# The first stretch of an attention + rational MLP + soft-MoE kernel: constants, two attention pairs and the first weight conversions put in an order written by hand, loads moved to one queue, one conversion operation moved from ScalarE to GpSimd

## The chip, the core and the metric

The kernel runs on one core of a Trainium2 chip. The metric is the device time in microseconds (us) of one execution; lower is better. The engines are TensorE (PE; PEld is its weight load), VectorE (DVE), ScalarE (ACT), GpSimd (POOL) and SyncE (SP, which here only issues DMA transfers). A name with q behind it (SPq, POOLq, ACTq) is that engine's instruction queue. Each engine takes its instructions strictly in its own order; an instruction whose inputs are not ready holds up everything behind it on that engine.

## What is computed

```python
# attention: 4 batches x 8 heads, 768 tokens in chunks of 32, head size 64
k_full = concat([mem_k, k[c_start - 16 : c_end + 8]])      # 64 keys for each chunk, v alike
a = softmax(q_c @ k_full.T / 8);  out_c = a @ v_full
x = attention output as [3072 tokens, 512]
# rational MLP: w_in 512 x 2048, w_out 2048 x 512; both come as float64
h = x @ w_in
g = (a0 + a1*h + a2*h**2 + a3*h**3) / (1 + |b0|*|h| + |b1|*h**2 + 1e-6)
y = g @ w_out
# soft MoE: 8 experts of 4 slots
logits = y @ phi;  slot inputs = softmax over tokens (logits).T @ y
slot outputs = relu(slot @ w1[e]) @ w2[e];  out = softmax over slots (logits) @ slot outputs
```

## The kernel before

The 3072 tokens go in six blocks of 512. A block holds two attention "pairs" of 256 tokens (the tiles `q`, `k`, `v`). For one pair PE makes the scores (L162), DVE takes the row maximum and subtracts it (L180, L183), ACT takes the exponential (L184), DVE sums and inverts (L187 to L189), PE transposes (L197), ACT copies (L199), PE multiplies by v (L207), DVE scales (L217), PE transposes (L226), and ACT and DVE write the result as a high part (L230) and a rest (L231) into the two `xt` tiles of the block. After that a block runs eight steps, one for each 256 columns of `w_in`: PE makes `h` with 24 matmuls (L310), and ACT, DVE and POOL compute the rational function (ACT L527, L528, L530, L546, L547; DVE L529, L540, L541, L557, L558; POOL L504). PE then transposes the result and adds the logits. There are 48 such steps; L529 is the first DVE instruction of a step and occurs once in each.

The two float64 weight matrices arrive as pairs of 32-bit words in eight chunks each, 1 MB a chunk, in staging tiles `g` (four buffers). The word i0 to i7 means the load of a chunk of `w_in`, o0 to o7 one of `w_out`. A conversion to float32 (`f64_narrow`) scales the low word (ACT L269), clips the high word (DVE L270), shifts its exponent (ACT L271) and joins both (DVE L272). For `w_in` (`split_w`, s0 to s7) ACT then makes the high part (L293) and DVE the rest (L294), into `win` tiles. For `w_out` (`narrow_w_out`, n0 to n7) the result goes to a scratch tile and from there to DRAM by a transfer that POOL issues (L301); PE and ACT then form its product with `phi` (w0 to w7: L405, L406; z0 to z7: L413, L414).

All conversions lie ahead of block 0 and in its eight steps. `KN['pre']` lists the work ahead of the first `h`: A and B are slices of the attention of pairs 0 and 1, the other words are loads and conversions. `KN['ord0']` lists the parts of a step of block 0 (s2, for instance, converts the chunk two steps ahead). The emission order gives priorities; a scheduler builds each engine's order from them.

The loads i0, i1, o0, o1 and all q, k, v loads are issued by SP; the later i and o loads by POOL (L280, L285), behind the stores of L301 in POOL's order.

Of the kernel before, what the change touches and what calls it, by code (L numbers as in the profile page):

```python
# [12 lines left out]
AF = mybir.ActivationFunctionType  # L13
ALU = mybir.AluOpType
AX = mybir.AxisListType
U32 = mybir.dt.uint32
# [3 lines left out]
def float_of_bits(u):  # L20
# [1 line left out]


KN = {
    'pre': "q0 i0 v0 q1 o0 v1 i1 o1 s0 A A A A A A A A A A n0 B B B B B B B B B B A A A A A A B B w0 B B B B i2 s1 o2 n1 z0 q2 v2 i3".split(),
    'ord0': "at a1 w1 s2 h0 d1 at t o3 z1 i4 n2 at a2 h1 p0 at p1 at at".split(),
    'ord': "at a1 h0 d1 at t a2 x2 h1 p0 p1 x1 at x3 at at".split(),
    'ordz': "d0 a1 t d1 a2 p0 p1".split(),
# [14 lines left out]
def tile_chunk_attention__rational__soft_moe(  # L43
# [15 lines left out]
    PE, ACT, DVE, POOL, SP = nc.tensor, nc.scalar, nc.vector, nc.gpsimd, nc.sync  # L59

    NPAIR, P, HP, _ = qw.shape
# [5 lines left out]
    NE, _, EFF = w1.shape  # L67
# [15 lines left out]
    LOW = 7.4 / 2.0 ** 32  # L83
    F64_HI = float_of_bits((1150 << 20) | 0xFFFFF)
    w_in = w_in.bitcast(U32)
    w_out = w_out.bitcast(U32)
# [4 lines left out]
    p_T = Pool(ctx.enter_context(tc.tile_pool(name="p_T", bufs=5)))  # L91
# [53 lines left out]
    def attention(pair, tile4=None, after=None):  # L145
        tile4 = tile4 or (lambda shape: p_a4("a4", shape))
        after = pair + 1 if after is None else after
        t_first = 2 * pair
        b = (t_first * P) // BLK
        qt, kt = ahead.pop(("q", pair))  # L150
        if pair < 2:
            both = ps_h("h", [P, 2, 2, HP, WIN])
            sc = [both[:, par] for par in range(2)]
        else:
            sc = [bank([P, 2, HP, WIN]) for _ in range(2)]
        for n in range(2):
            for hp in range(HP):
                for c in range(4):
                    for par in range(2):
                        r = slice(D * par, D * par + D)  # L160
                        o = P * n + CH * c
                        PE.matmul(  # L162
                            sc[par][CH * c:CH * c + CH, n, hp, :],
                            lhsT=qt[r, hp, o:o + CH],
                            rhs=kt[r, hp, 4 * n + c, :],
                            start=True, stop=True)
            yield
        if after < NPAIR:
            load_qk(after)
        pr = tile4([P, 2, HP, 2, WIN])  # L170
        rsum = []
        for par in range(2):
            for n in range(2):
                s0 = ((t_first + n) % TPB) * P
                if s0 == 0:
                    DVE.memset(sc[par][0:CH, n, :, 0:LEFT], NEG)
                if s0 + P == S:
                    DVE.memset(sc[par][P - CH:P, n, :, CTX - RIGHT:CTX], NEG)
            mx = p_sm("mx", [P, 2, HP], bufs=2)
            DVE.tensor_reduce(mx, sc[par], AX.X, ALU.max)  # L180
            yield
            e = pr[:, :, :, par, :]
            DVE.tensor_tensor(e, sc[par], mx.unsqueeze(3).to_broadcast([P, 2, HP, WIN]), ALU.subtract)  # L183
            ACT.activation(e, e, AF.Exp, scale=SCALE)  # L184
            yield
            sm = p_sm("sm", [P, 2, HP], bufs=4)
            DVE.tensor_reduce(sm, e, AX.X, ALU.add)  # L187
            DVE.tensor_scalar(sm, sm, 1e-9, None, ALU.add)
            DVE.reciprocal(sm, sm)  # L189
            rsum.append(sm)  # L190
            yield

        pt = tile4([P, 2, HP, P])
        for n in range(2):
            pb = bank([P, HP, P])
            for hp in range(HP):
                PE.transpose(pb[:, hp, :], pr[:, n, hp].rearrange("p a j -> p (a j)"), ident)  # L197
            yield
            ACT.activation(pt[:, n], pb, AF.Copy)  # L199
        vt = ahead.pop(("v", pair))  # L200
        pv = [bank([P, 2, HP, D]) for _ in range(2)]
        for n in range(2):
            for hp in range(HP):
                for c in range(4):
                    for par in range(2):
                        r = slice(WIN * par, WIN * par + WIN)
                        PE.matmul(  # L207
                            pv[par][CH * c:CH * c + CH, n, hp, :],
                            lhsT=pt[r, n, hp, CH * c:CH * c + CH],
                            rhs=vt[n][r, c, hp, :],  # L210
                            start=True, stop=True)
            if n and after < NPAIR:
                load_v(after)
            yield
        x_tok = tile4([P, 2, HP, 2, D])
        for par in range(2):
            DVE.tensor_tensor(x_tok[:, :, :, par, :], pv[par],  # L217
                              rsum[par].unsqueeze(3).to_broadcast([P, 2, HP, D]), ALU.mult)
            yield

        xh, xl = xt[b]
        for n in range(2):
            o = (P // TT) * ((t_first + n) % TT)
            pb = bank([P, HP, P])
            for hp in range(HP):
                PE.transpose(pb[:, hp, :], x_tok[:, n, hp].rearrange("p a d -> p (a d)"), ident)  # L226
            yield
            src = pb.rearrange("p h (r t) -> p h t r", t=TT)
            th, tl = (x.rearrange("p h (t r) -> p h t r", t=TT)[:, :, :, o:o + P // TT] for x in (xh, xl))
            ACT.activation(th, src, AF.Copy)  # L230
            DVE.tensor_tensor(tl, src, th.bitcast(F32), ALU.subtract)  # L231
            yield

    def attention_block(b):
        new_xt(b)
        for n in range(BLK // (2 * P)):
            yield from attention(b * BLK // (2 * P) + n)

    make_identity(nc, ident)
    ACT.dma_start(out=ctab[:, 0:4], in_=ca.unsqueeze(0).to_broadcast([P, 4]))  # L240
    ACT.dma_start(out=ctab[:, 4:6], in_=cb.unsqueeze(0).to_broadcast([P, 2]))
# [20 lines left out]
    def f64_narrow(dst, src):  # L262

        lo, hi = src[:, :, :, 0], src[:, :, :, 1]
        f = hi.bitcast(F32)
        ACT.activation(lo, lo, AF.Copy, scale=LOW)  # L269
        DVE.tensor_scalar(f, f, -F64_HI, F64_HI, ALU.max, ALU.min)  # L270
        ACT.activation(f, f, AF.Prelu, scale=2.0 ** -112, alpha=-(2.0 ** 32))  # L271
        DVE.scalar_tensor_tensor(dst, hi, 3, lo, ALU.logical_shift_left, ALU.bitwise_or)  # L272

    stage_in, stage_out = {}, {}
    scratch = [p_win("win", [P, 1024]) for _ in range(3)]
# [1 line left out]

    def load_w_in(i):
        t = p_g("g", [P, NC, 2 * P, 2], U32)
        (SP if i < 2 else POOL).dma_start(out=t.rearrange("p c f w -> p c (f w)"), in_=w_in[i])  # L280
        stage_in[i] = t

    def load_w_out(i):
        t = p_g("g", [P, 2, DM, 2], U32)
        (SP if i < 2 else POOL).dma_start(out=t.rearrange("p c f w -> p c (f w)"), in_=w_out[i])  # L285
        stage_out[i] = t

    def split_w(i):
        wh, wl = win[i] = [p_win("win", [P, NC, 2 * P], F32R) for _ in range(2)]
        src = stage_in.pop(i)  # L290
        f64_narrow(src[:, :, :, 1], src)
        f = src[:, :, :, 1].bitcast(F32)
        ACT.activation(wh, f, AF.Copy)  # L293
        DVE.tensor_tensor(wl, f, wh.bitcast(F32), ALU.subtract)  # L294
# [2 lines left out]

    def narrow_w_out(i):
        f = scratch[i % 3].rearrange("p (j d) -> p j d", j=2)
        f64_narrow(f.bitcast(U32), stage_out.pop(i))  # L300
        POOL.dma_start(out=wo_dr[i], in_=f)  # L301
        wo[i] = f

# [117 lines left out]
    def load(what):  # L421
        kind, n = what[0], int(what[1])
        if kind == "q":
            if n == 1:
                load_qk(1, early["q"], early["k"])
            else:
                load_qk(n)
        elif kind == "v":
            load_v(n, [p_S("S", [P, 4, HP, D]) for _ in range(2)] if n == 1 else None)
        elif kind == "i":  # L430
            load_w_in(n)
        elif kind == "o":
            load_w_out(n)

    def convert(what):
        kind, n = what[0], int(what[1])
        if n < NSTEP:
            {"s": split_w, "n": narrow_w_out, "w": wp_chunk, "z": wp_sum, "i": load_w_in, "o": load_w_out}[kind](n)

    new_xt(0)  # L440
    pairs = {"A": attention(0, after=NPAIR), "B": attention(1, lambda shape: p_T("T", shape), after=NPAIR)}
    for what in KN["pre"]:
        if what in pairs:
            next(pairs[what], None)
        elif what[0] in "qmv":
            load(what)
        else:
            convert(what)
    for gen in pairs.values():
        for _ in gen:  # L450
            pass
    total = NBLK * NSTEP
    hs, gt_tile = {}, {}

# [116 lines left out]
    for kk in range(total + 4):  # L571
        b, i = divmod(kk, NSTEP)
# [31 lines left out]
    for n in range(4):  # L604
        for j in range(4):
# [3 lines left out]
                      start=(n == 0), stop=(n == 3))  # L609
# [132 lines left out]
```

## Time and profile before

| | before |
|---|---|
| device time, median of 3 runs | 609.6 us (608.68 to 610.11) |
| the profiled execution: own time / span of its trace | 611.2 / 609.3 us |
| PE, DVE, ACT, POOL busy | 542.0, 450.9, 419.0, 131.0 us |
| granted TensorE clock, mean of the span | 0.959 of full speed |

The span runs from the first instruction to the last of the profiled execution, which as a whole took 1.9 us longer than its span and 1.6 us longer than the median of the timed runs. The busy time of PE counts modelled ends of pipelined matmuls. DMA issue and semaphore instructions are not counted as busy.

### The profile page before, as it was taken

What the parts mean: (1) busy time and instruction counts of PE and PEld (TensorE: products, weight loads), DVE (VectorE), ACT (ScalarE), POOL (GpSimd) and SP (SyncE); (2) the same over time, 40 slices, a digit from 0 to 9 for tenths busy, and PEclk for the clock granted to TensorE, in tenths of its full rate; (3) what the DMA queues carried; (4) which work ended last, traced back from release to release, by engine and by line L of the source; (5) the groups of instructions that cost most, each with busy time, mean ns of one, the idle gap of its engine ahead of it and who ended that gap; (6) DMA issues with size and microseconds to landing.
All of it is one profiled execution on the core that took longest, in us unless ns stands there. A gap on an engine that the chain in (4) does not pass through costs nothing.

```text
span 609.3 us, 13452 instructions
## 1 busy us (share of the span) xinstructions
PE 542.0 (89%) x5832; PEld 380.4 (62%) x5832; DVE 450.9 (74%) x559; ACT 419.0 (69%) x542; POOL 131.0 (21%) x77
## 2 busy tenths in 40 slices
PE   1247999999999999999999999999999998879981
PEld 1236887766776777767777677776777575326220
DVE  3775698985997888979889798897987969710031
ACT  2576799987786787878867778687787869410041
POOL 0111132122331321312313223132233215100000
PEclk9865999999999999999999999999999999788996
DMA  8995953330201322112221032210274344799938
GB/s 304 415 364 236 342 177 121 136 126 35 105 12 61 104 71 105 30 42 105 71 104 49 23 104 72 104 63 10 104 275 161 119 137 161 289 365 400 411 146 335
DMA packets 21755, 97.41 MB, mean 160 GB/s; under 512 B 3136, under 2 KB 3136, under 8 KB 16704
## 3 DMA queue, kind: packets, MB, share of 16 engines
q1 hardware_dynamic: 18000, 79.70, 35.0%
q0 software_dynamic: 2880, 16.78, 7.4%
q8 instruction: 46, 0.75, 0.5%
q10 hardware_dynamic: 816, 0.07, 0.1%
q14 instruction: 13, 0.11, 0.1%
HBM read 86.05 MB, written 10.49 MB: 158 GB/s over the span
## 4 chain that ended last, share of the span: by engine, by line
PE 56%; ACT 12%; DVE 12%; issue 9%; DMA 6%; POOL 2%; DVEq 0%; ACTq 0%; POOLq 0%; SPq 0%
PE h L310 29%; PE m L336 4%; PE m L387 4%; PE lg L329 3%; ACT S L527 3%; DMA g<-in_moe_w_in_dram 3%; ACT S L528 3%; PE m L207 2%; DVE T L540 2%; ACT g L337 2%; PE h L627 2%; PE m L413 2%; POOL S L504 2%; PE m L226 2%; DVE T L541 2%
## 5 line engine op out<-in xcount | busy, mean ns | idle before, releaser
L310 PE MATMUL h<-xt,win 128*128 128x512 f32 x1152 | 292.0, 401 | 0.7 <-DVE T L541 0.6
L310 PEld LDWEIGHTS h<-xt,win 128*128 128x128 f32 x1152 | 209.7, 189 | 46.1 <-DVE T L541 1.4
L504 POOL TENSOR_TENSOR S<-S,S 128x1024 f32<-128x1024 f32 (+1 forms) x49 | 118.1, 2413 | 306.6 <-DVE S L529 282.0
L527 ACT ACTIVATE S<-h,ctab 128x1024 f32<-128x1024 f32 (+1 forms) x49 | 53.8, 1099 | 55.7 <-PE h L310 54.1
L529 DVE SCALAR_TENSOR_TENSOR S<-S,S 128x1024 f32<-128x1024 f32 (+1 forms) x49 | 58.9, 1201 | 40.7 <-ACT S L528 40.6
L540 DVE TENSOR_TENSOR T<-T,h 128x1024 f32<-128x1024 f32 (+1 forms) x49 | 58.4, 1191 | 7.0 <-ACT T L530 7.0
L557 DVE SCALAR_TENSOR_TENSOR T<-T,ctab,S 128x1024 f32<-128x1024 f32 (+1 forms) x49 | 63.3, 1293 | 0.0
L558 DVE SCALAR_TENSOR_TENSOR T<-S,T 128x1024 f32<-128x1024 f32 (+1 forms) x49 | 59.8, 1220 | 3.3 <-POOL S L504 0.5
L336 PEld LDWEIGHTS m<-ident,T 128*128 128x128 f32 x384 | 44.3, 144 | 28.2 <-issue 13.8
L541 DVE SCALAR_TENSOR_TENSOR T<-T,ctab,h 128x1024 f32<-128x1024 f32 (+1 forms) x49 | 61.1, 1246 | 1.1 <-DVE T L540 0.4
L530 ACT ACTIVATE T<-h,ctab 128x1024 f32<-128x1024 f32 (+1 forms) x49 | 59.2, 1208 | 0.0
L337 ACT ACTIVATE g<-m 128x512 f32<-128x512 f32 x96 | 53.6, 603 | 6.4 <-PE m L336 5.2
L546 ACT ACTIVATE S<-S 128x1024 f32<-128x1024 f32 (+1 forms) x49 | 51.7, 1056 | 8.6 <-DVE S L529 5.1
L547 ACT ACTIVATE S<-S,ctab 128x1024 f32<-128x1024 f32 (+1 forms) x49 | 55.9, 1141 | 0.8
L336 PE MATMUL m<-ident,T 128*128 128x128 f32 x384 | 54.1, 281 | 1.2 <-DVE a L183 1.2
L528 ACT ACTIVATE S<-h,ctab 128x1024 f32<-128x1024 f32 (+1 forms) x49 | 54.1, 1105 | 0.4 <-DVE T L557 0.4
L329 PE MATMUL lg<-T,wp 128*32 128x512 f32 x192 | 38.5, 618 | 3.9 <-DVE T L558 3.8
L231 DVE TENSOR_TENSOR xt<-m,xt 128x512 fp32r<-128x512 f32 x24 | 16.5, 688 | 13.9 <-ACT xt L230 13.9
L387 PE MATMUL m<-g,ptok 128*32 128x512 f32 x192 | 23.5, 634 | 0.4 <-ACT ptok L379 0.4
L269 ACT ACTIVATE g<-g 128x1024 uint32<-128x1024 uint32 x16 | 18.6, 1161 | 6.5 <-DMA g<-in_moe_w_in_dram 5.0
L680 DVE TENSOR_SCALAR win<-h,csum 128x512 f32<-128x512 f32 x12 | 8.0, 744 | 20.3 <-PE m L674 20.3
L184 ACT ACTIVATE a<-a 128x512 f32<-128x512 f32 x22 | 14.0, 636 | 12.6 <-DVE a L183 12.6
(154 smaller groups left out, 611.7 us busy)
## 6 DMA issues: line engine op xcount, KB each, us to landing
win<-in_moe_w_dram SPq DMA_DIRECT2D x32, 512.0 KB, 4.9
k<-in_kw_dram SPq DMA_DIRECT2D x11, 1024.0 KB, 7.0
v<-in_vw_dram SPq DMA_DIRECT2D x11, 1024.0 KB, 4.9
g<-in_moe_w_in_dram POOLq DMA_DIRECT2D x6, 1024.0 KB, 7.8
g<-in_moe_w_out_dram POOLq DMA_DIRECT2D x6, 1024.0 KB, 9.6
out_dram<-win SPq DMA_DIRECT2D x12, 512.0 KB, 6.2
q<-in_qw_dram SPq DMA_DIRECT2D x11, 512.0 KB, 3.8
T<-in_moe_w_dram SPq DMA_DIRECT2D x10, 512.0 KB, 10.0
```

Source lines behind the costliest of these rows:

```text
L310: PE.matmul(tile_[:, f2, :], lhsT=ww[:, c, f2 * P:f2 * P + P], rhs=xx[:, c, :], start=(n == 0), stop=(n == 3 * NC - 1))
L336: PE.transpose(pb[:, m, f2 * P:f2 * P + P], t_[:, f2, tt * P:tt * P + P], ident)
L337: ACT.activation(gts[b, qd][:, 2 * part:2 * part + 2, 2 * P * o:2 * P * o + 2 * P], pb, AF.Copy)
L504: POOL.tensor_tensor(out[:, o], q[:, o], w[:, o], ALU.mult)
L527: ACT.activation(s[:, o], hh[:, o], AF.Abs, scale=b0)
L528: ACT.activation(y[:, o], hh[:, o], AF.Square, scale=rb1)
L529: DVE.scalar_tensor_tensor(s[:, o], y[:, o], QC, s[:, o], ALU.add, ALU.add)
L530: ACT.activation(t[:, o], hh[:, o], AF.Identity, bias=a2, scale=a3)
L540: DVE.tensor_tensor(t[:, o], t[:, o], hh[:, o], ALU.mult)
L541: behind[kk] = DVE.scalar_tensor_tensor(t[:, o], t[:, o], a1, hh[:, o], ALU.add, ALU.mult).ins
L557: DVE.scalar_tensor_tensor(t[:, o], t[:, o], a0, w[:, o], ALU.add, ALU.mult)
L558: DVE.scalar_tensor_tensor(t[:, o], e[:, o], 2.0, t[:, o], ALU.subtract, ALU.mult, reverse0=True)
```

## The change

It has four parts. First, everything from the constants to the first `h` is written in a fixed order for PE, ACT, DVE and POOL (`manual_schedule`), in which the slices of pairs 0 and 1 (A, B), the conversion s0 (s) and n0 (n) stand as `KN['pre']` lists them. The conversions became generators for that, in two slices each. What remains of the old list (s1, w0, z0, n1 and the loads i2, o2, i3) is `KN['pre2']`, behind the fixed part and left to the scheduler. Second, the first loads are issued in the order of `KN['loads']`, and all i and o loads are issued by SP. Third, the low words are scaled by POOL in place of ACT, in all 16 conversions. Fourth, in every attention pair the two row sums come after both exponentials.

```diff
 KN = {
-    'pre': "q0 i0 v0 q1 o0 v1 i1 o1 s0 A A A A A A A A A A n0 B B B B B B B B B B A A A A A A B B w0 B B B B i2 s1 o2 n1 z0 q2 v2 i3".split(),
+    'loads': "q0 q1 v0 i0 v1 o0 i1 o1 q2 v2".split(),
+    'pre': "A A B B A A A A A A A A A A B B B B s B B B B A A B B s A A A A s n B B n B B B B".split(),
+    'pre2': "s1 i2 w0 z0 o2 n1 i3".split(),
...
             ACT.activation(e, e, AF.Exp, scale=SCALE)
             yield
+        for par in range(2):
             sm = p_sm("sm", [P, 2, HP], bufs=4)
-            DVE.tensor_reduce(sm, e, AX.X, ALU.add)
+            DVE.tensor_reduce(sm, pr[:, :, :, par, :], AX.X, ALU.add)
...
+    start = ExitStack()
+    start.enter_context(tc.manual_schedule(engines={e.engine for e in (PE, ACT, DVE, POOL)}))
     make_identity(nc, ident)
...
-        ACT.activation(lo, lo, AF.Copy, scale=LOW)
+        POOL.tensor_scalar(lo, lo, LOW, None, ALU.mult)
         DVE.tensor_scalar(f, f, -F64_HI, F64_HI, ALU.max, ALU.min)
         ACT.activation(f, f, AF.Prelu, scale=2.0 ** -112, alpha=-(2.0 ** 32))
+        yield
         DVE.scalar_tensor_tensor(dst, hi, 3, lo, ALU.logical_shift_left, ALU.bitwise_or)
+        yield
...
-        (SP if i < 2 else POOL).dma_start(out=t.rearrange("p c f w -> p c (f w)"), in_=w_in[i])
+        SP.dma_start(out=t.rearrange("p c f w -> p c (f w)"), in_=w_in[i])
...
-        (SP if i < 2 else POOL).dma_start(out=t.rearrange("p c f w -> p c (f w)"), in_=w_out[i])
+        SP.dma_start(out=t.rearrange("p c f w -> p c (f w)"), in_=w_out[i])
...
     new_xt(0)
-    pairs = {"A": attention(0, after=NPAIR), "B": attention(1, lambda shape: p_T("T", shape), after=NPAIR)}
+    for what in KN["loads"]:
+        load(what)
+    gens = {"A": attention(0, after=NPAIR), "B": attention(1, lambda shape: p_T("T", shape), after=NPAIR),
+            "s": split_w(0), "n": narrow_w_out(0)}
     for what in KN["pre"]:
-        if what in pairs:
-            next(pairs[what], None)
-        elif what[0] in "qmv":
-            load(what)
-        else:
-            convert(what)
-    for gen in pairs.values():
+        next(gens[what], None)
+    for gen in gens.values():
         for _ in gen:
             pass
+    start.close()
+    for what in KN["pre2"]:
+        load(what) if what[0] in "qv" else convert(what)
```

The lines move down by 2 to 9 in the changed kernel: L269 becomes L274 (now on POOL), L270 L275, L271 L276, L272 L278, L293 L300, L294 L301, L301 L308, L310 L317, L217 L220, L230 L233, L231 L234, L406 L413, L414 L421, L504 L513, L527 L536, L529 L538.

ACT's order before, from the middle of the first stretch to the high parts of `xt` (L230 into xt_3; a4 and T are the probabilities of pairs 0 and 1; g_5 holds chunk i2, g_6 o2, g_7 i3):

```order
L269 ACTIVATE g_5_540<-g_5_540 128x1024
L271 ACTIVATE g_5_540<-g_5_540 128x1024
L269 ACTIVATE g_6_550<-g_6_550 128x1024
L230 ACTIVATE xt_3_148<-m_7_443 128x16x32
L293 ACTIVATE win_8_670<-g_5_540 128x1024
L271 ACTIVATE g_6_550<-g_6_550 128x1024
L269 ACTIVATE g_7_573<-g_7_573 128x1024
L406 ACTIVATE S_3_517<-m_10_518 128x512
L406 ACTIVATE S_3_517<-m_11_524 128x512
L230 ACTIVATE xt_3_148<-m_12_533 128x16x32
L271 ACTIVATE g_7_573<-g_7_573 128x1024
L414 ACTIVATE wp_4_106<-m_13_557 128x64
```

The last two L230 stand behind the last row. ACT's order now, at the same place (g_1 holds i0, g_2 o0, g_3 i1):

```order
L202 ACTIVATE T_2_428<-m_5_429 128x512
L202 ACTIVATE T_2_428<-m_6_435 128x512
L233 ACTIVATE xt_3_150<-m_9_511 128x16x32
L233 ACTIVATE xt_3_150<-m_10_518 128x16x32
L300 ACTIVATE win_4_415<-g_1_160 128x1024
L276 ACTIVATE g_3_168<-g_3_168 128x1024
L276 ACTIVATE g_2_166<-g_2_166 128x1024
L233 ACTIVATE xt_3_150<-m_11_534 128x16x32
L233 ACTIVATE xt_3_150<-m_12_541 128x16x32
```

All four high parts stand ahead of every operation on i2, o2 and i3, which are no longer ahead of them at all; o0 and i1 still are.

DVE's order now, from pair 0's scaling to the first instruction of step 0 (L538):

```order
L278 SCALAR_TENSOR_TENSOR g_1_160<-g_1_160 128x1024
L234 TENSOR_TENSOR xt_4_151<-m_9_511,xt_3_150 128x16x32
L275 TENSOR_SCALAR g_3_168<-g_3_168 128x1024
L234 TENSOR_TENSOR xt_4_151<-m_10_518,xt_3_150 128x16x32
L301 TENSOR_TENSOR win_5_416<-g_1_160,win_4_415 128x1024
L275 TENSOR_SCALAR g_2_166<-g_2_166 128x1024
L220 TENSOR_TENSOR T_3_530<-m_7_444,sm_7_420 128x8x64
L220 TENSOR_TENSOR T_3_530<-m_8_445,sm_8_424 128x8x64
L278 SCALAR_TENSOR_TENSOR win_1_145<-g_2_166 128x1024
L278 SCALAR_TENSOR_TENSOR g_3_168<-g_3_168 128x1024
L234 TENSOR_TENSOR xt_4_151<-m_11_534,xt_3_150 128x16x32
L234 TENSOR_TENSOR xt_4_151<-m_12_541,xt_3_150 128x16x32
```

The last L234 ends the inputs of the first `h`. Counted to step 0's L538, DVE has done 13 conversion instructions (6 clips, 5 joins, 2 rests) of the 40 that all chunks need; before, 24 (10, 9 and 5) stood ahead of step 0's L529. So 27 are left for the steps of block 0 (10 clips, 11 joins, 6 rests) where 16 were (6, 7 and 3), and 10 scalings are left for POOL.

POOL's order now, in the first steps of block 0 (S are the operands of the multiplication of L513, win the scratch tiles that L308 stores):

```order
L274 TENSOR_SCALAR g_7_590<-g_7_590 128x1024
L274 TENSOR_SCALAR g_8_728<-g_8_728 128x1024
L308 DMA wo_1_144<-win_3_147 128x1024
L274 TENSOR_SCALAR g_9_740<-g_9_740 128x1024
L513 TENSOR_TENSOR S_9_783<-S_4_653,S_7_755 128x1024
L274 TENSOR_SCALAR g_10_831<-g_10_831 128x1024
L308 DMA wo_1_144<-win_1_145 128x1024
L513 TENSOR_TENSOR S_13_950<-S_8_781,S_11_856 128x1024
```

Each step of block 0 now has two scalings beside the one multiplication and the one store; the load issues are gone from POOL.

## Rows read from the trace of the kernel before

**Rows 1.** Page: busy us, share of the span and instructions by engine.

```profile
PE 542.0 (89%) x5832; PEld 380.4 (62%) x5832; DVE 450.9 (74%) x559; ACT 419.0 (69%) x542; POOL 131.0 (21%) x77
```

**Rows 2.** Stages: start:end, length, busy us (instructions) per engine, clock, DMA share, GB/s.

```profile
30.00:40.00 10.00, 3.77 (x136) 3.28 (x136) 6.57 (x11) 7.76 (x9) 0.69 (x2) 0.67 0.99 400
50.00:60.00 10.00, 10.00 (x76) 8.32 (x78) 5.42 (x7) 6.77 (x10) 0.00 (x0) 0.50 0.44 180
```

**Rows 3.** Chain that ended last, in order of time: start us, us, what.

```profile
26.58 0.58 POOL wo L301
...
27.30 9.27 DMA g<-in_moe_w_in_dram
...
38.72 8.55 DMA g<-in_moe_w_in_dram
...
47.36 1.17 ACT g L269
...
57.44 2.43 PE h L310 x5
```

**Rows 4.** Timeline: start us, us, engine, line, operation, out<-in, idle before and releaser.

```profile
8.99 2.04 PE L162 MATMUL h<-k,q 64*32 64x64 f32 x128 [8.99 <-DMA k<-in_kw_dram]
18.79 0.33 SPq L280 DMA_DIRECT2D g<-in_moe_w_in_dram  x1
19.12 0.42 PE L162 MATMUL h<-xt,xt 64*32 64x64 f32 x2 [8.09 <-DMA xt<-in_kw_dram]
21.59 0.70 DVE L270 TENSOR_SCALAR g<-g 128x1024 f32<-128x1024 f32 x1 [0.18 <-DMA g<-in_moe_w_out_dram]
50.86 3.62 PE L413 MATMUL m<-u,S 128*128 128x32 f32 x16
67.81 1.23 DVE L529 SCALAR_TENSOR_TENSOR S<-S,S 128x1024 f32<-128x1024 f32 x1 [2.02 <-ACT S L528]
151.73 1.23 DVE L529 SCALAR_TENSOR_TENSOR S<-S,S 128x1024 f32<-128x1024 f32 x1 [3.38 <-ACT S L528]
```

**Rows 5.** Who waited, SP's queue: total us, times, longest us.

```profile
SPq L280 <- DMA u<-in_moe_phi_dram: 9.1, 1, 9.1
```

**Rows 6.** Stages as in Rows 2: step 0 to step 7, and block 1.

```profile
67.81:151.73 83.92, 80.39 (x877) 62.72 (x876) 71.76 (x82) 73.47 (x96) 19.47 (x13) 1.00 0.41 148
148.59:232.16 83.57, 83.30 (x941) 60.60 (x947) 70.22 (x82) 65.49 (x83) 21.67 (x9) 1.00 0.19 64
```

**Rows 7.** Groups by line and shape: count, busy us, mean ns, idle before.

```profile
L504 POOL TENSOR_TENSOR S<-S,S 128x1024 f32<-128x1024 f32 x47 | 115.1, 2451 | 300.0 <-DVE S L529 282.0 <-DVE sm L189 10.5 <-DVE ce L368 7.5
L269 ACT ACTIVATE g<-g 128x1024 uint32<-128x1024 uint32 x16 | 18.6, 1161 | 6.5 <-DMA g<-in_moe_w_in_dram 5.0 <-DMA g<-in_moe_w_out_dram 1.5
L270 DVE TENSOR_SCALAR g<-g 128x1024 f32<-128x1024 f32 x16 | 11.0, 690 | 3.5 <-DMA g<-in_moe_w_in_dram 3.3 <-DMA g<-in_moe_w_out_dram 0.2
L272 DVE SCALAR_TENSOR_TENSOR g<-g 128x1024 uint32<-128x1024 uint32 x8 | 9.8, 1222 | 1.1 <-ACT g L271 1.0
```

**Rows 8.** One line, L617: min/median/max ns.

```profile
L617 POOL MEMSET a<- x1: 952/952/952, 544.0 to 544.0; 128x1024 f32 x1
```

**Rows 9.** Timeline as in Rows 4, three meetings of DVE and POOL.

```profile
79.90 1.22 DVE L540 TENSOR_TENSOR T<-T,h 128x1024 f32<-128x1024 f32 x1
80.07 2.39 POOL L504 TENSOR_TENSOR S<-S,S 128x1024 f32<-128x1024 f32 x1 [0.67 <-DVE S L529]
81.03 1.46 DVE L188 TENSOR_SCALAR sm<-sm 128x8 f32<-128x8 f32 x1
...
123.66 2.71 POOL L504 TENSOR_TENSOR S<-S,S 128x1024 f32<-128x1024 f32 x1 [4.89 <-DVE S L529]
124.44 3.01 DVE L272 SCALAR_TENSOR_TENSOR win<-g 128x1024 uint32<-128x1024 uint32 x1 [0.34 <-ACT g L271]
...
142.14 1.22 DVE L294 TENSOR_TENSOR win<-g,win 128x1024 fp32r<-128x1024 f32 x1
142.38 3.23 POOL L504 TENSOR_TENSOR S<-S,S 128x1024 f32<-128x1024 f32 x1 [5.47 <-DVE S L529]
```

More of the change, by code (lines that the diff above doesn't have):

```diff
@@ L290, in split_w @@
         src = stage_in.pop(i)
-        f64_narrow(src[:, :, :, 1], src)
+        yield from f64_narrow(src[:, :, :, 1], src)
         f = src[:, :, :, 1].bitcast(F32)
@@ L299, in narrow_w_out @@
         f = scratch[i % 3].rearrange("p (j d) -> p j d", j=2)
-        f64_narrow(f.bitcast(U32), stage_out.pop(i))
+        yield from f64_narrow(f.bitcast(U32), stage_out.pop(i))
         POOL.dma_start(out=wo_dr[i], in_=f)
@@ L437, in convert @@
         if n < NSTEP:
-            {"s": split_w, "n": narrow_w_out, "w": wp_chunk, "z": wp_sum, "i": load_w_in, "o": load_w_out}[kind](n)
+            for _ in {"s": split_w, "n": narrow_w_out, "w": wp_chunk, "z": wp_sum, "i": load_w_in, "o": load_w_out}[kind](n) or ():
+                pass
     new_xt(0)
-    pairs = {"A": attention(0, after=NPAIR), "B": attention(1, lambda shape: p_T("T", shape), after=NPAIR)}
+    for what in KN["loads"]:
+        load(what)
+    gens = {"A": attention(0, after=NPAIR), "B": attention(1, lambda shape: p_T("T", shape), after=NPAIR),
+            "s": split_w(0), "n": narrow_w_out(0)}
     for what in KN["pre"]:
-        if what in pairs:
-            next(pairs[what], None)
-        elif what[0] in "qmv":
-            load(what)
-        else:
-            convert(what)
-    for gen in pairs.values():
+        next(gens[what], None)
+    for gen in gens.values():
         for _ in gen:
             pass
+    start.close()
+    for what in KN["pre2"]:
+        load(what) if what[0] in "qv" else convert(what)
     total = NBLK * NSTEP
```

## The prediction

> **What bounds the kernel now.** I read the page first. PE is busy 542.0 of 609.3 us and DVE 450.9 [rows 1], so a gain must come where PE does not work. The stages show where: from 30 to 40 us PE is busy 3.77 of 10, and the first matmul of `h` starts at 57.4 [rows 2, 3]. The chain of waits tells why. POOL issues its first store only at 26.58, because DVE has not joined o0 sooner; chunk i2, behind it on POOL, then takes 9.27 us to land, chunk i3, issued at 38.72, another 8.55, and ACT L269 on i3 runs at 47.36 [rows 3]. None of that is needed by the first `h`, but on ACT and DVE these operations stand ahead of the last pieces of `xt`. The reader is to see a stretch that waits for transfers of later steps.
>
> From step 0's L529 at 67.81 to step 7's at 151.73 [rows 4] it is another picture: of 83.92 us PE is busy 80.39, ACT 73.47 and DVE 71.76 [rows 6]. Block 1 has PE busy 83.30 of 83.57 [rows 6]. From step 0 on PE sets the pace, with DVE at 86% in block 0. Whatever is won ahead of step 0 shifts all that follows, unless block 0 gets longer.
>
> **When step 0 can come.** The transfers set the earliest times. With 1.57 MB (q0, k0) landed PE starts at 8.99, with 5.24 MB queued up to k1 at 19.12, with o0 as the next 1.05 MB DVE starts at 21.59 [rows 4]: 2.5 us for each further MB. The bytes up to a place in the new order give k1 13, v0 16, i0 19, v1 21.6, o0 24, i1 27, as estimates from these rows. The issue of i1 waits for the small table of `phi` as before (9.1 us, issued at 18.79 [rows 4, 5]); by then 7.3 MB stand ahead of it, so I add nothing.
>
> On DVE pair 0's maxima, subtractions and sums go from 11 to 16, pair 1's to about 23 with the clip of i0 between, which comes at 19 and may stand behind POOL's scaling of i0. The scaling of pair 0 follows at 23 to 25. PE then does pair 1's product with v and the four groups of transposes; the rest is a ladder of ACT copies and DVE subtractions of 0.6 to 0.7 us each, with the clips and joins of i0, i1 and o0 between (0.69 and 1.22 us each [rows 7]). All of it lies behind i1's landing at 27. Counting the rows of DVE's and ACT's new order one behind the other, the last `xt` piece is ready at 37 to 38. I take 38 for the first `h` in place of 57.4, 19.4 us sooner, with 36 and 42 as ends.
>
> From there to L529 it took 10.4 us (57.4 to 67.81 [rows 3, 4]). Now w0 and z0, done earlier before, stand between the matmuls of step 0; z0's sixteen took 3.62 us at the low clock [rows 4] (0.50 of full, which is 1.2 GHz, from 50 to 60 [rows 2]), and some thirty small score matmuls of pair 2 move out from between them. I add 2.4. Step 0's L538 comes at about 51, **17 us sooner** (13 to 20).
>
> **What block 0 gives back.** The conversions that were done in the 57 us of waiting come later now: in DVE's new order 10 clips, 11 joins and 6 rests are left behind step 0's L538, where 6, 7 and 3 were. These are 4 x 0.69 and 7 x 1.22 [rows 7] = 11.3 us more; back to back they overlap by 0.1 each, so 10.4. DVE's 71.76 become 82.2 of 83.9. ACT loses seven L269 and gains four L271 and three L293, each about 1.16 [rows 7]: nothing. PE does the same.
>
> Then the scalings on POOL, 10 of them in this stretch. The trace has no such operation. Below it lies a POOL write of 1024 elements without a read, 0.95 us [rows 8]; above it one with two reads, 2.45 us [rows 7]. One read and one write lie between: 1.7. POOL has room (19.47 busy of 83.92 [rows 6], 36 then), and twelve load issues leave it. But POOL and DVE hold each other up. DVE L188, an operation on 8 elements a row, took 1.46 and ended at 82.49, as POOL's multiplication at 82.46; the join at 124.44 took 3.01, its own 1.22 behind the end of a multiplication at 126.37; and POOL's at 142.38 took 3.23, since L294 ran to 143.36 [rows 9]. L540, which reads one operand from PSUM, kept its 1.22 beside the first of these multiplications [rows 9]. I take the clip, the join and the rest for such operations, and L529, L557 and L558 too: 10 x 0.69, 17 x 1.22 and 21 x 1.23 [rows 4, 7] are about two thirds of the 82.2. A scaling that comes at a random moment waits or makes DVE wait; I put half its time on DVE, 0.85 us each, 8.5 in all. The ends are nothing (it falls beside L540 and L541 or an idle DVE) and all of 2.45.
>
> The Trainium skill, SBUF — State Buffer, section "SBUF: two separate sides", says that a DVE operation with two SBUF inputs or in a two-port mode and a GpSimd operation exclude each other for the whole instruction. The three meetings agree with it; by the rule alone each scaling could cost DVE its full length, which is the rival below that ends slower. The GPSIMD Engine Reference of the Trainium skill, section "Engine selection", calls one-input operations roughly line-rate; from its 1.2 GHz that would be an estimate of 0.85 us for 1024 elements, and at half of it the give-back would be some 4 us smaller. No row here shows a one-input operation of this size.
>
> DVE needs 82.2 + 8.5 = 90.7 then, more than PE's 80.4, and sets the pace. It will not run without a gap, PE needed 4% more than its busy time; I take 92. Block 0 gives back 92 - 84 = **8 us**.
>
> **The other edits.** The sums behind both exponentials take as many instructions in as many slices; they fill DVE while ACT works, in steps where PE is the bound (83.30 of 83.57 in block 1 [rows 6]): nothing. The joins now also wait for POOL; queued behind a late scaling are a store and the multiplication of L513, for which the end of a step waits. Scalings start when their chunk lands, and the slots of `g` come free about a step (10 us) ahead of use, so I cost this at nothing; without that lead each would put its own 1.7 us and a wait for landing on the step. On SP the loads now stand behind q3, k3 and v3, which wait for PE's use of pair 2; the same step of lead covers them, and without it a load's landing, about 9 us [rows 3], would fall on the step.
>
> **Sum.** 17 sooner less 8 is 9. The profiled execution took 611.2 (span 609.3 and 1.9 around it), so it would take 602.2, the span 600.3. The median of the runs is 1.6 below the profiled one: **600.6 us**.
>
> **Rivals.**
> 1. *The scalings are cheap* (25%). If a scaling is near 0.95 us and finds DVE in its PSUM operations, DVE stays near 84 and PE keeps the pace. For it: L540 was not held up [rows 9]. Against it: DVE then is at 98%. Block 0 gives back 1 to 2: 594, between 591 and 596.
> 2. *The scalings stop DVE* (10%). One mechanism: DVE's clip, join or first step operation stands behind every scaling for its whole length. At 2.45 us each DVE needs 82.2 + 24.5 = 106.7, block 0 gives back 22.8, and the time is 615. It decides from 17 = 82.2 + 10x - 83.9, x = 1.87 us each. For it: two of the three meetings are of this kind [rows 9]. Against it: POOL also waits for DVE, and a multiplication, longer by every row, kept DVE only in part.
> 3. *Step 0 hardly comes sooner* (10%). DVE's fixed order has the clip of i1 ahead of pair 0's last piece and that of o0 ahead of pair 1's scaling. If i1 lands at 33 instead of 27, everything behind it moves 6 us: 17 becomes 11, and the time 606.6. For it: fixed orders cannot step around a late transfer. Against it: as many bytes stand ahead of i1 as before.
>
> **Numbers.** The main case has 55%, 597 to 605. The range leaves out the far side of rival 2 and the lower edge of rival 1: 591 to 608.5. A measurement of this kernel tells some 0.2% from no change, so faster means below 608.4. The main case, rival 1 and nearly all of rival 3 are faster, 0.90; 0.03 lie within 0.2%; rival 2 from its point on and a late start together with it are slower, 0.07.
>
> **What would show it.** In the changed kernel's trace: L317 starting near 38 and step 0's L538 near 51; no wait of ACT or DVE for i2 or i3 ahead of it; L274 between 0.95 and 2.45 us; from step 0's to step 7's L538 some 92 us, with DVE busy over 95% and DVE operations of twice their length beside L274; block 1 as long as before. I am wrong if that stretch stays at 84 or goes beyond 101, or if L317 starts after 45.

## The result, and the profile after

The change made the kernel slower: 614.36 us (median of 4 runs, 613.47 to 615.21) against 609.86 (4 runs, 608.68 to 610.18), a ratio of 1.0084 with a 95% interval of 1.0072 to 1.0096. The forecast, 600.6 us and faster, was wrong in sign; 614.36 lies outside its range. The profiled execution took 614.46 us, with a span of 612.7.

The page of the changed kernel, busy time by engine, answers to [rows 1]:

```profile
PE 544.5 (89%) x5832; PEld 382.3 (62%) x5832; DVE 461.4 (75%) x559; ACT 403.0 (66%) x526; POOL 177.3 (29%) x81
```

POOL has 46 us more and ACT 16 less, as the edit says; DVE has 10.5 more with the same 559 instructions. The timeline of the changed kernel, with the first `h` matmul and the first DVE instruction of steps 0 and 7, answers to [rows 4]:

```profile
41.31 0.80 PE L317 MATMUL h<-xt,win 128*128 128x512 f32 x1
...
52.23 1.21 DVE L538 SCALAR_TENSOR_TENSOR S<-S,S 128x1024 f32<-128x1024 f32 x1
...
155.46 1.23 DVE L538 SCALAR_TENSOR_TENSOR S<-S,S 128x1024 f32<-128x1024 f32 x1 [4.79 <-ACT S L537]
```

Step 0 comes 15.6 us sooner (67.81 before), step 7 comes 3.7 us later (151.73 before). Everything that was won ahead of step 0 is lost between these two rows, and more. The stages of the changed kernel, columns as in [rows 2]: from step 0 to step 7 (called the stretch from here on), and on to the first instruction of the last step:

```profile
52.23:155.46 103.23, 88.37 (x879) 68.38 (x878) 88.78 (x93) 74.24 (x96) 54.08 (x23) 0.93 0.48 166
155.46:525.02 369.56, 361.79 (x3846) 262.52 (x3844) 318.39 (x360) 289.03 (x367) 99.59 (x41) 1.00 0.27 93
```

The stretch takes 103.23 us where it took 83.92 [rows 6]. The rest, 369.56, hardly moved: before, 368.86 from step 7's L529 at 151.73 to the last at 520.59. In the stretch DVE executes 93 instructions (82 before) and is busy 88.78 us, close to the 90.7 of the forecast; yet the stretch is 103, not 92. The scaling itself, one line over the whole kernel:

```profile
L274 POOL TENSOR_SCALAR g<-g x16: 2874/3010/3982, 19.3 to 128.7; 128x1024 uint32<-128x1024 uint32 x16
```

Its median of 3.01 us lies above the bracket of 0.95 to 2.45. Three meetings of it with DVE, from the timeline of the changed kernel:

```profile
62.27 1.22 DVE L538 SCALAR_TENSOR_TENSOR S<-S,S 128x1024 f32<-128x1024 f32 x1
62.65 3.63 POOL L274 TENSOR_SCALAR g<-g 128x1024 uint32<-128x1024 uint32 x1 [2.22 <-ACT a L186]
...
99.17 2.97 POOL L274 TENSOR_SCALAR g<-g 128x1024 uint32<-128x1024 uint32 x1
101.22 1.23 DVE L301 TENSOR_TENSOR win<-g,win 128x1024 fp32r<-128x1024 f32 x1 [3.16 <-ACT win L300]
...
108.42 2.95 POOL L274 TENSOR_SCALAR g<-g 128x1024 uint32<-128x1024 uint32 x1
108.54 2.08 DVE L538 SCALAR_TENSOR_TENSOR S<-S,S 128x1024 f32<-128x1024 f32 x1
```

At 62.65 the scaling takes 0.6 us more than its median beside L538, which had begun; at 101.22 L301, with two operands in SBUF, keeps its 1.23 us inside a scaling; at 108.54 L538 is held up for 0.86 and ends at 110.62, before the scaling does (111.37). Either side can pay, with a part of the other's length or with nothing. The Trainium skill, SBUF — State Buffer, section "SBUF: two separate sides", gives whichever of the two begins first the shared port for the whole instruction. The first meeting can be read so; the other two, by their recorded spans, differ from it, and the measurement decides here.

The waits of the changed kernel in the stretch, by engine and line (us in total, times, longest us):

```profile
ACT S L555 <- POOL S L513: 7.9, 4, 3.1
...
PE h L317 <- ACT win L300: 3.7, 3, 2.0
```

Before, L546 (now L555) waited 3.5 us for the multiplication in the stretch, and no `h` matmul for `win`. Rows of the chain that ended last in the changed kernel, in order of time as in [rows 3]:

```profile
77.44 9.01 DMA g<-in_moe_w_out_dram
...
86.59 2.94 POOL g L274
...
95.70 1.84 POOL S L513
...
111.45 2.37 POOL S L513
...
127.86 6.73 DMA wo<-win
```

From the load at 77.44 to L555's start at 113.84 the chain lies on that load and on POOL's order alone: four scalings, two stores and two multiplications, with the gaps between them. In the two longest gaps (1.9 and 5.6 us) a store waited for a join on DVE. The last row is a store. Its join ended on DVE at 125.69; the store stands behind L513 in POOL's order, goes out at 127.86 and takes 6.73 us, and the next high part (L300) waits 3.1 us for the `win` slot that the store reads. In all, 23.4 us of the stretch's chain are on POOL, 15.7 on transfers, 20.5 on PE, 15.7 on ACT, 13.6 on DVE, and for 14.4, those two gaps among them, the chain names no engine.

### The profile page after: what moved, and what is told of

It is laid out like the page before. It is cut to its first block, busy times and chain, and to the rows that moved or that the text cites. A ratio compares the mean times of both kernels' runs of the same rounds, so it can differ in the third digit from the quotient of the medians.

```text
span 612.7 us, 13472 instructions
## 1 busy us (share of the span) xinstructions
PE 544.5 (89%) x5832; PEld 382.3 (62%) x5832; DVE 461.4 (75%) x559; ACT 403.0 (66%) x526; POOL 177.3 (29%) x81
## 4 chain that ended last, share of the span: by engine, by line
PE 49%; DVE 13%; ACT 13%; DMA 9%; issue 7%; POOL 6%; SPq 0%; DVEq 0%; ACTq 0%; POOLq 0%
PE h L317 26%; PE m L394 4%; POOL S L513 3%; ACT S L536 3%; PE m L343 3%; DMA win<-in_moe_w_dram 3%; PE m L210 3%; ACT g L344 3%; ACT S L537 3%; PE lg L336 3%; DVE T L549 2%; POOL g L274 2%; PE m L229 2%; PE m L200 2%; DMA xt<-in_kw_dram 2%
## 5 line engine op out<-in xcount | busy, mean ns | idle before, releaser
L317 PE MATMUL h<-xt,win 128*128 128x512 f32 x1152 | 294.0, 404 | 4.7 <-ACT win L300 3.7
L317 PEld LDWEIGHTS h<-xt,win 128*128 128x128 f32 x1152 | 212.3, 191 | 51.8 <-ACT win L300 5.0
L513 POOL TENSOR_TENSOR S<-S,S 128x1024 f32<-128x1024 f32 (+1 forms) x49 | 119.0, 2431 | 296.1 <-DVE S L538 289.3
L536 ACT ACTIVATE S<-h,ctab 128x1024 f32<-128x1024 f32 (+1 forms) x49 | 53.8, 1099 | 62.3 <-PE h L317 60.3
L538 DVE SCALAR_TENSOR_TENSOR S<-S,S 128x1024 f32<-128x1024 f32 (+1 forms) x49 | 59.6, 1217 | 40.4 <-ACT S L537 40.2
L555 ACT ACTIVATE S<-S 128x1024 f32<-128x1024 f32 (+1 forms) x49 | 51.7, 1054 | 12.9 <-POOL S L513 7.9
L274 POOL TENSOR_SCALAR g<-g 128x1024 uint32<-128x1024 uint32 x16 | 51.5, 3221 | 25.2 <-DMA g<-in_moe_w_in_dram 18.0
L234 DVE TENSOR_TENSOR xt<-m,xt 128x512 fp32r<-128x512 f32 x24 | 16.4, 687 | 13.0 <-ACT xt L233 13.0
L210 PE MATMUL m<-v,a 64*32 64x64 f32 x1408 | 21.8, 236 | 4.2 <-issue 2.5
L210 PEld LDWEIGHTS m<-v,a 64*32 64x32 f32 x1408 | 18.1, 112 | 9.1 <-issue 4.8
```

The lines of the kernel that those rows point to most:

```text
L274: POOL.tensor_scalar(lo, lo, LOW, None, ALU.mult)
L317: PE.matmul(tile_[:, f2, :], lhsT=ww[:, c, f2 * P:f2 * P + P], rhs=xx[:, c, :], start=(n == 0), stop=(n == 3 * NC - 1))
L513: POOL.tensor_tensor(out[:, o], q[:, o], w[:, o], ALU.mult)
L536: ACT.activation(s[:, o], hh[:, o], AF.Abs, scale=b0)
L538: DVE.scalar_tensor_tensor(s[:, o], y[:, o], QC, s[:, o], ALU.add, ALU.add)
```

## The experiments

All 14 kernels ran on a chip beside the kernel before, whose median was between 608.7 and 609.2 in each batch. "Stretch" and busy times are those of one profiled execution. The kernels marked * spread by 1.2% to 1.7% between executions, e5 and e13 by about 1%, so a stretch of theirs is good to a few us. The profiled execution of e5 was 4.1 us above its median, that of e11 2.5 above, that of e6 2.3 below. "Fuller" is the larger busy share of DVE and ACT in the stretch.

| kernel | median us | ratio, 95% interval | step 0 at | stretch | PE / DVE / ACT busy in it | fuller |
|---|---|---|---|---|---|---|
| before | | | 67.81 | 83.92 | 80.39 / 71.76 / 73.47 | ACT 0.88 |
| after | 614.36 | 1.0084 [1.0072, 1.0096] | 52.23 | 103.23 | 88.37 / 88.78 / 74.24 | DVE 0.86 |
| e1_act_scale | 608.21 | 0.9985 [0.9967, 1.0004] | 52.81 | 95.58 | 87.33 / 83.07 / 84.63 | ACT 0.89 |
| e2_before_pool | 616.37 | 1.0122 [1.0096, 1.0149] | 60.79 | 96.79 | 87.18 / 78.04 / 69.20 | DVE 0.81 |
| e3_hybrid | 608.45 | 0.9988 [0.9971, 1.0005] | 52.76 | 97.96 | 89.16 / 83.64 / 84.63 | ACT 0.86 |
| e5_dve_shift | 615.82 | 1.0121 [1.0075, 1.0168] | 57.17 | 103.43 | 92.01 / 90.31 / 74.49 | DVE 0.87 |
| e7_no_clip * | 607.29 | 0.9959 [0.9929, 0.9989] | 52.68 | 94.58 | 86.07 / 75.64 / 85.44 | ACT 0.90 |
| e8_no_scale | 605.57 | 0.9939 [0.9919, 0.9959] | 52.34 | 92.12 | 85.15 / 84.45 / 74.20 | DVE 0.92 |
| e6_act_poolloads * | 605.78 | 0.9942 [0.9912, 0.9972] | 53.00 | 90.99 | 85.11 / 80.72 / 82.45 | ACT 0.91 |
| e10_before_noclip | 603.93 | 0.9917 [0.9892, 0.9942] | 64.74 | 79.84 | 78.54 / 66.19 / 72.75 | ACT 0.91 |
| e11_pool_both | 622.46 | 1.0222 [1.0187, 1.0257] | 54.53 | 110.56 | 91.86 / 88.19 / 73.17 | DVE 0.80 |
| e12_before_sp | 606.56 | 0.9963 [0.9939, 0.9987] | 58.95 | 89.97 | 85.58 / 79.89 / 79.06 | DVE 0.89 |
| e13_sums_before | 603.87 | 0.9917 [0.9888, 0.9947] | 53.28 | 92.62 | 84.66 / 81.53 / 81.49 | DVE 0.88 |
| e14_poolloads_noclip | 602.28 | 0.9894 [0.9878, 0.9911] | 51.49 | 88.86 | 82.60 / 72.78 / 82.50 | ACT 0.93 |
| e16_neither | 600.66 | 0.9858 [0.9838, 0.9878] | 51.98 | 87.27 | 85.24 / 74.46 / 73.28 | DVE 0.85 |
| e15_before_2scale * | 614.28 | 1.0079 [1.0047, 1.0111] | 63.47 | 93.43 | 84.48 / 74.10 / 84.50 | ACT 0.90 |

**The scaling or the conversions left over.** The first theory, P, was that the scalings on POOL cause the loss; its rival, L, that the conversions left for block 0 do. e1 takes the scaling back to ACT and keeps the rest of the change:

```diff
-        POOL.tensor_scalar(lo, lo, LOW, None, ALU.mult)
+        ACT.activation(lo, lo, AF.Copy, scale=LOW)
```

> The changed kernel with the low words scaled by ACT again (part three undone, all else kept). Theory P (the ten 3.0 us scalings on POOL make block 0 long, by POOL's order and by stopping DVE): step 0's L538 stays near 52 us, the stretch to step 7's falls from 103 to between 84 and 95 (DVE 82 + 4, ACT 74 + 12), the time is 596 to 607. Theory L (27 conversion instructions of DVE left for block 0 make it long on whatever engine the scaling is): the stretch stays above 99 and the time is 611 to 615.

e2 makes the opposite edit in the kernel before and nothing else. e3 leaves POOL only the scalings of s0 and n0 in the fixed part. e5 puts the scaling on DVE as a shift to the right (it cuts off where the scaling rounds):

```diff
-        POOL.tensor_scalar(lo, lo, LOW, None, ALU.mult)
+        DVE.tensor_scalar(lo, lo, 29, None, ALU.logical_shift_right)
```

> The kernel before with only the scaling moved to POOL (part three alone). Theory P: the first matmul of h moves little or comes a few us later, the stretch from step 0's L529 to step 7's grows from 84 to 90 or more, the time is 616 to 625. Theory L: the order before leaves 16 conversion instructions for block 0 and has ACT relieved, so the stretch stays within 3 us of 84 and the time is 607 to 612.

> The changed kernel with POOL scaling only s0 and n0 in the fixed part, ACT all 14 later chunks. Theory P: as with ACT alone, within 3 us, since POOL has no other work so early: 595 to 607, no POOL operation but L513's in block 0. Theory L: 611 to 615.

> The changed kernel with the low words brought to three bits by DVE, with a shift right by 29 in place of the scaling (it cuts off where the scaling rounds). POOL is as free as with ACT, DVE has ten more instructions of 0.7 to 1.2 us in block 0. Theory P: DVE then sets the pace with 82 + 4 + 7 to 12, the stretch is 93 to 99, the time 602 to 609. Theory L: DVE's load is what counts, the stretch is over 103 and the time 614 or more. The duration of the shift is also looked for.

Both theories hold in part: e2 came out as P said, e5 as L said, e1 and e3 just outside P's ranges. Without POOL's scalings the stretch still takes 95.58 us, 11.7 more than before, at 608.21 us: all else in the change together is worth nothing that can be measured. POOL's scalings add another 7.6 us, and alone they make the kernel before slower by 1.2%, though step 0 comes 7.0 us sooner there, which no theory had. In the fixed part they are free: e3 equals e1.

With e1's instruction count within one, DVE is busy 88.78 - 83.07 = 5.7 us longer in the changed kernel: about 0.6 us for each of the ten scalings. In e5 POOL scales nothing, DVE does 90.31 us of work, and the stretch is as long as in the changed kernel, in an execution 4.1 us above the median. Here work added to DVE costs about its own length (7.2 us more work than in e1, 7.9 more stretch); the forecast had 92 for 90.7.

**Is it DVE's work alone?** The busy share of DVE was 0.85 to 0.87 in every kernel of these but e2, which suggested that its work sets the stretch (theory D). e7 is e1 without the clip, e10 the kernel before without it:

```diff
-        DVE.tensor_scalar(f, f, -F64_HI, F64_HI, ALU.max, ALU.min)
```

> The changed kernel with ScalarE's scaling of the low words and without VectorE's clip of the high words (the clipping of weights beyond float32's range is left out). It takes 14 clips of about 0.69 us, 9.7 us, from VectorE between step 0's and step 7's L538. Theory D (VectorE's work sets that stretch, at about 0.86 of it busy in every kernel so far): VectorE falls from 83.1 to 73.4 us, the stretch from 95.6 to 85 to 88 us, the time from 608.2 to 598 to 601 us. Theory A (ScalarE's 84.6 us or TensorE's 87.3 us in that stretch set it): the stretch stays at 93 to 96 us, the time at 606 to 609 us.

> The kernel before without VectorE's clip of the high words (the clipping is left out). It takes some 10 clips, 6.9 us, from VectorE between step 0's and step 7's L529. Theory D by its rule of 0.86: VectorE falls from 71.8 to 64.9 us, but TensorE's 80.4 us is a floor, so the stretch goes from 83.9 to 80 to 82 us and the time falls by 2 to 4 us. Theory A (TensorE already sets the kernel before's stretch): the stretch stays at 83 to 84 us, and the time falls by 1 us at most, for the clips ahead of step 0.

e8 is the changed kernel without any scaling; the join reads a zero (`none`) in place of the low word, which is left out:

```diff
+    zero = const("zero", [P, 1])
...
+    POOL.memset(zero, 0.0)
...
-        POOL.tensor_scalar(lo, lo, LOW, None, ALU.mult)
+        none = zero.bitcast(U32).unsqueeze(2).to_broadcast(list(hi.shape))
...
-        DVE.scalar_tensor_tensor(dst, hi, 3, lo, ALU.logical_shift_left, ALU.bitwise_or)
+        DVE.scalar_tensor_tensor(dst, hi, 3, none, ALU.logical_shift_left, ALU.bitwise_or)
```

> The changed kernel with no scaling of the low words at all (the low words are left out; the join reads a zero in their place, with the same VectorE instruction). GpSimd has the load of the kernel before, ScalarE some 10 us less than with its own scaling, VectorE the same conversions. Theory D: the stretch from step 0's to step 7's L538 is as with ScalarE's scaling, 94 to 97 us, and the time 606 to 609 us. Theory A, by ScalarE: the stretch falls to 86 to 90 us and the time to 599 to 603 us.

Theory D fell with e7: DVE lost 7.4 us of the stretch's work, the stretch 1.0. Theory A, by ScalarE alone, fell with e8: ACT lost 10.4, the stretch 3.5 where at least 5.6 was expected. e10 came out just below the lower end of D's stretch (79.84), with PE busy 78.54 of it, and gained 3.1 ahead of step 0 besides; its time fell by 5.0 us for the 2 to 4 expected.

e8 also splits the loss. In the stretch it has the changed kernel's instructions on DVE (93) and ACT (96) and no scaling. It takes 92.12 us, 8.2 more than before: that is what the moved conversions cost, with the loads on SP and the sums as changed. The ten scalings on POOL make the other 11.1 us of the changed kernel's stretch and 8.8 us of its median (614.36 beside 605.57), and DVE is busy only 4.3 us longer with them. In the chain of e8's stretch, as in that of e1's, nothing lies on POOL or on a transfer.

**The queue of the loads.** e6 is e1 with the loads from the third chunk on issued by POOL, e11 the changed kernel with them there, e12 the kernel before with all of them on SP; in both load functions:

```diff
-        SP.dma_start(out=t.rearrange("p c f w -> p c (f w)"), in_=w_in[i])
+        (SP if i < 2 else POOL).dma_start(out=t.rearrange("p c f w -> p c (f w)"), in_=w_in[i])
```

> The changed kernel with ScalarE's scaling and with the weight loads from the third on issued by GpSimd, as in the kernel before. Theory D: the queue does not matter, the stretch is 94 to 97 us and the time 606 to 609 us. Rival Q (loads issued by SP wait behind other work of SP, so conversions come late): the stretch is 90 us or less and the time 603 us or less.

> The changed kernel, GpSimd scaling and all, with the weight loads from the third on issued by GpSimd as in the kernel before. Theory Q (the issue by SP puts the conversions of the next chunks later in the orders that the scheduler builds, so TensorE waits for win, at a cost of its own): the stretch from step 0's to step 7's L538 is 4 to 5 us shorter than in the changed kernel, 98 to 100 us, with no wait of L317 for win, and the time 608 to 611 us. Rival (on GpSimd the loads stand behind the 3.0 us scalings and come as late): the stretch stays at 102 us or more and the time at 613 us or more.

> The kernel before with all weight loads issued by SP and nothing else changed. Theory Q: as in the changed kernel, 4 to 5 us worse: the stretch from step 0's to step 7's L529 goes from 83.9 to 87 to 90 us, the time to 611 to 615 us. Rival (the queue costs only where step 0 comes early and little lead is left): stretch and time as before within 1 us, or shorter ahead of step 0, because i2 and i3 no longer stand behind the first store.

In e6 no matmul of `h` waits for `win` as it does in e1 (2.5 us), and chunk i4 is issued at 52.51 instead of 56.93. The stretch is 4.6 us shorter in the profiled runs, the median 2.4 us lower; the intervals of the two ratios overlap at their ends, and neither theory's ranges were met. Chunk i4 goes out when the rest (L301) of i2 frees its slot, and in e1 that rest stands behind two instructions of step 0, in e6 ahead of them. This is the order that the scheduler built; why it builds another one when the issuer changes, the trace does not show.

With POOL scaling, the same edit costs 8 us instead. The waits of e11 in the stretch:

```profile
POOL g L287 <- issue: 7.5, 2, 6.5
POOL g L274 <- DMA g<-in_moe_w_in_dram: 7.5, 2, 5.9
```

Loads stand behind scalings and scalings wait for loads, in one order on one engine. e2 has both on POOL too; these two are the only kernels where the fuller engine is near 0.80. Theory Q fell here: where POOL scales, SP is the better issuer. e12 was expected slower by Q, and equal or sooner ahead of step 0 by the rival; it came out 0.4% faster: step 0 comes 8.9 us sooner, since i2 and i3 no longer wait for the first store, and the stretch gives back 6.0, with DVE at 79.89 of work for 71.76. It is the changed kernel's exchange on a small scale.

**The sums, and what is left.** e13 is e6 with each row sum right behind its own exponential, e14 is e6 without the clip:

```diff
-        for par in range(2):
             sm = p_sm("sm", [P, 2, HP], bufs=4)
-            DVE.tensor_reduce(sm, pr[:, :, :, par, :], AX.X, ALU.add)
+            DVE.tensor_reduce(sm, e, AX.X, ALU.add)
```

> The kernel with ScalarE's scaling and GpSimd's issue of the later loads, and with each row sum right behind its own exponential, as in the kernel before. If the order of the sums costs nothing, as forecast: 603 to 608 us, the first h at 41 to 42.5 us, the stretch 90 to 92 us. Rival: the sums behind both exponentials are worth a gain in the fixed part, and the first h comes 1 us or more later here.

> The kernel with ScalarE's scaling and GpSimd's issue of the later loads, without VectorE's clip (the clipping is left out). Theory W (once no matmul waits for win, VectorE's moved conversions are what is left of the give-back): 14 clips of 0.69 us less, VectorE 72 us busy, the stretch falls from 91.0 to 82 to 85 us and the time to 595 to 599 us. Rival (the order of the conversions alone sets it): the stretch stays at 89 to 92 us and the time at 602 to 606 us.

The sums make no difference that these runs can tell: e13's 0.9917 and e6's 0.9942 have overlapping intervals. Theory W was wrong: 8 us less DVE work shortened the stretch by 2, not 6 to 9, and the time fell where the rival had it; ACT stood at 0.93.

**Both at once, and ACT doubled.** The column "fuller" gave the last theory, E: DVE and ACT feed each other, and whichever has more to do can be busy at most about 0.9 of the stretch. It would explain why taking from one of them moves the end to the other. e16 is e8 without the clip; e15 adds to the kernel before a second, idle scaling:

```diff
         ACT.activation(lo, lo, AF.Copy, scale=LOW)
+        ACT.activation(lo, lo, AF.Copy, scale=1.0)
```

> The changed kernel without the scaling of the low words and without the clip (both left out). Each alone hardly shortened the stretch from step 0's to step 7's L538: without the clip 94.6 us, without the scaling 92.1, with both 95.6. Theory E (whichever of VectorE and ScalarE is the fuller sets the stretch, at 0.86 to 0.93 of it busy; without the clip that was ScalarE, without the scaling VectorE): VectorE has 76 us left and ScalarE 74, the stretch falls to 82 to 88 us, and the time to 594 to 600 us. Rival O (the order and the lateness of the conversions set it, whatever their length): the stretch stays at 90 to 94 us and the time at 602 to 607 us.

> The kernel before with every low word scaled twice by ScalarE, the second time by 1. It puts 10 operations of about 1.06 us more on ScalarE between step 0's and step 7's L529. Theory E: ScalarE goes from 73.5 to 84 us and becomes the fuller engine, the stretch from 83.9 to 91 to 97 us, the time to 616 to 622 us. Theory D (VectorE alone sets it) and rival O: the stretch stays at 83 to 87 us, and the time rises to at most 613 us.

Without the clip alone the median of e1 falls by 0.9 us, without the scaling alone by 2.6, without both by 7.5: one edit alone leaves the other engine's work. In e16 PE is busy 85.24 of 87.27 and sets the pace again. In e15 ACT's 11 us more lengthen the stretch by 9.5, though DVE had room; the share is 0.90. Both stretches are as E says and not as its rivals; the times lie 0.7 us above (e16) and 1.7 below (e15) their ranges. In e15 step 0 came 4.3 us sooner than in the kernel before, which no theory had and which stays open. Of the 9.5 us, 8.2 lie in step 4 (17.88 us for 9.73), where DVE stood 5.63 us until a load of `w_out` landed at 129.66. The L530 behind it was released by ACT 0.61 us after that, so the load is not the whole of it, but how much of the 9.5 is the late load stays open.

What these two runs show is that ACT's added work alone lengthens the stretch, and that relieving both engines shortens it where relieving one hardly does. They do not show a ceiling of 0.9: the share is an average over seven unlike steps, and in single steps DVE and ACT reach 0.97 to 1.00 (below).

## Why the forecast was wrong

1. *When step 0 can come*: right. L317 at 41.31 is inside 36 to 42, L538 at 52.23 beside 51, 15.6 us sooner for 17. The first `h` came 3.3 us later than the 38, and the way on to L538 took 10.9 us for 12.8: two misses that partly cancel. Rival 3 is out.
2. *The conversions left for block 0*: right in count, 11 instructions more on DVE. The 82.2 us without scalings is 83.07 in e1 and 84.45 in e8.
3. *The price of a scaling*: POOL's own time was outside the bracket (3.01 us median), and further from the estimate of 0.85. The price on DVE was inside: 0.4 us each beside e8, 0.6 beside e1, for 0.85. Rival 2 named the right time, 615, by a mechanism that was not there: it needed 1.87 us each.
4. ***DVE sets the pace, I take 92* for 90.7 is the step that failed.** DVE's work was nearly right (88.78). The gap beside it was put at 1.3 us, and the margin of 4% that the prediction names would have made 94.7; measured, DVE was idle for 14.45 us of 103.23. The steps show where. Columns as in [rows 2], the changed kernel's steps 1 to 6, then the last two of the kernel before:

```profile
62.27:77.30 15.03, 13.24 (x189) 10.31 (x187) 14.56 (x18) 12.51 (x16) 9.65 (x3) 1.00 0.63 233
77.30:91.62 14.32, 11.94 (x182) 8.68 (x182) 14.13 (x14) 10.82 (x13) 10.34 (x5) 1.00 0.74 247
91.62:108.54 16.92, 13.86 (x72) 9.74 (x73) 13.52 (x16) 10.71 (x13) 11.03 (x6) 1.00 0.70 248
108.54:123.34 14.80, 11.83 (x123) 9.66 (x124) 14.80 (x19) 12.24 (x18) 5.19 (x2) 0.80 0.19 57
123.34:141.96 18.62, 15.57 (x147) 11.16 (x145) 14.65 (x14) 12.16 (x18) 7.54 (x4) 0.98 0.39 130
141.96:155.46 13.50, 11.90 (x51) 10.35 (x52) 7.19 (x6) 7.40 (x11) 2.35 (x1) 0.75 0.09 33
```

```profile
122.26:141.00 18.74, 17.23 (x152) 11.31 (x150) 14.45 (x14) 15.71 (x21) 3.85 (x3) 1.00 0.33 122
141.00:151.73 10.73, 9.65 (x55) 7.91 (x54) 7.20 (x7) 7.42 (x11) 3.23 (x1) 1.00 0.00 0
```

In steps 1, 2 and 4 DVE is busy 0.97 to 1.00, in step 0 0.99; in steps 3, 5 and 6 it is 0.80, 0.79 and 0.53, and 13.7 of its 14.45 idle us lie there. The last two steps held little DVE work before the change as well (0.77 and 0.67). The forecast compared one engine's total with the length of the stretch, as if the work lay evenly in it. But the moved conversions fall into steps that DVE already fills, and the room in the last steps is no use to them. Without any scaling (e8) DVE is busy 0.99 to 1.00 in steps 2 to 4 and the stretch 8.2 us longer, where the forecast's 82.2 alone would have cost next to nothing (rival 1 has 1 to 2 us).
5. *ACT loses seven and gains seven: nothing*. Right for the changed kernel: 96 instructions as before, 74.24 us for 73.47. With the scaling back on it (e1) ACT was the fuller engine and the stretch 95.58: the moved conversions, scalings included, eat 11.7 of the 15.0 us that step 0 comes sooner there. *PE does the same* was right in matmuls (879 for 877) and not in time: 88.37 us for 80.39, at a mean clock of 0.93 for 1.00. How much of the 19.3 us the clock makes, no run isolates.
6. *Queued behind a late scaling: nothing*. This failed too. The lead of a step was not there: the load at 77.44 went out when a join had just freed its slot (chain: L278 on DVE to 77.39), landed at 86.45, and its scaling began at 86.59; three times L513 began right behind a scaling (66.36, 95.70, 111.45), and L555's waits for L513 grew from 3.5 to 7.9 us. This is the case that the prediction names and costs at nothing. The scalings' 11.1 us (e8) are thus 4.3 us of longer DVE work and waits in POOL's order. Up to 92 us DVE worked beside that chain with hardly a gap, so how much each of the two makes is not shown.
7. *Loads on SP: nothing*. Wrong, with both signs: some 2.4 us too many beside ACT's scaling (e6, barely clear of noise), 8.1 saved beside POOL's (e11).
8. *The sums: nothing*, and block 1 and later as before: right.

The gain was not lost on the way to step 0. The conversions that had filled a wait were moved behind it, into steps in which DVE was already busy 0.84 to 1.00 (steps 0 to 4 before), and the scalings into a queue whose other work the steps wait for. The version that keeps the early start, scales on ACT and issues the later loads from POOL beats both kernels: 605.78 (e6) and 603.87 us (e13), the latter 0.9917 of before.

## What to carry to other kernels

Work that fills a wait is free there and paid for wherever it goes next. Before moving it, add it to the busy time of every engine in the new place, and step by step: an engine that is busy 0.86 of a stretch on average can be full in half of its steps. An operation that waits for a transfer, put into an in-order queue, holds up what stands behind it; cost that at nothing only if the trace shows the lead. Don't put transfers and the operations that wait for them into one in-order queue.

## What was not expected of the hardware

A POOL operation with one input took longer than one with two: 3.01 us (median, 128x1024 uint32, in place) against 2.43 for L513 (mean, float32). And the granted TensorE clock fell behind a gap of PE. In step 4 of the changed kernel (the row 108.54:123.34 above) it is 0.80 on average: 1.00 up to 116 us, and 0.50, the lower level of 1.2 GHz, from 118 us on. From 114 to 118 us PE was busy 1.48 of 4 us. Over the whole stretch the clock is 0.93, and nearly the same matmuls (879 and 877) take 88.37 us instead of 80.39. No run isolates the clock, but PE's busy time is not the fixed 80.4 us that the forecast took it for.
